# High and low parts written in natural token order, with the un-interleaving moved to the copies of the sums

## The chip, the cores and the metric

The kernel runs on one core of a Trainium2 chip. The metric is the device time of one execution in microseconds, and the median of several executions is compared. One profiled execution gives the trace in which all durations of this text stand. The engines are named as the profile names them: PE (TensorE, with PEld for its weight loads), DVE (VectorE), ACT (ScalarE), POOL (GpSimd) and SP (SyncE, which issues DMAs).

## What is computed

An attention over channels is followed by two feed-forward layers over 6016 tokens of 256 channels, with 2048 hidden channels each:

```python
def _attn_ref(q, k, v, tau):                # B, N, C = 1, 6016, 256
    qn = q / (np.linalg.norm(q, axis=1, keepdims=True) + 1e-06)
    kn = k / (np.linalg.norm(k, axis=1, keepdims=True) + 1e-06)
    s = kn.transpose(0, 2, 1) @ qn / tau
    s = s - s.max(-1, keepdims=True)
    a = np.exp(s)
    a /= a.sum(-1, keepdims=True) + 1e-09
    return (v @ a).astype(np.float32)

x = attn_out.reshape(6016, 256)
h = x @ w_in;   x = (h * np.cos(h)) @ w_out                  # first layer
h = x @ w_in2;  out = (h * (1 / (1 + np.exp(-h)))) @ w_out2  # second layer
```

## The kernel before

**Stages.** A prologue (the first 70 us or so) forms the scores and folds the attention matrix into the first layer's input weights. Then come the two layers. The tokens are cut into 12 blocks, four of 512 tokens and then eight of 496, in this order in both layers, and the hidden channels into 8 pairs of 128-channel slices. A block and a pair make a unit, so each layer has 96 units.

**High and low parts.** Every operand of a matmul is held as two fp32r tensors, the high part (a rounded copy) and the low part (what the rounding left), and a product is three matmuls: weights high by data high, weights low by data high, weights high by data low. For each unit ACT writes the high part and DVE subtracts it to get the low part.

**First layer, per unit.** PE makes `h` (12 matmuls, line 392). ACT takes the turns of the cosine's argument (L404), DVE reduces it (L405), ACT takes the sine (L412), DVE multiplies (L413) and has the product `t`. One unit later ACT writes `hi` from `t` (L420) and DVE writes `lo` (L421). PE uses them two units later, in 12 matmuls that add to the block's sum `o` in PSUM (L433). The order on each engine is the order of the code; ACT's is L404 of this unit, L420 of the last, L412 of this, and DVE's is L405, L421, L413. Between them stand the decoding of weights (L136 on ACT, L140 to L144 on DVE, L137 to L160 on POOL), the splitting of the next block's input on POOL (L213, L216), and the steps by which the last block's sum becomes the second layer's input.

**Between the layers.** `emit_x2` copies a finished sum out of PSUM (L470, ACT, both channel halves in one instruction), forms four combinations of its quarters, splits all seven forms into `yhi` and `ylo` (L454, L457), and stores them to DRAM.

**Second layer, per unit.** Products follow Winograd's form of Strassen's scheme: 2 x 2 blocks, seven products instead of eight, on half-blocks of 256 or 248 tokens. A unit costs 21 matmuls into `xz` and `ys` and 21 into the block's sums `o` (all L500). ACT applies Silu (L760, L771, L772) and copies seeds (L730, L731, L774). DVE adds (L719, L720) and forms combinations (L443, L448, and L449 on POOL). Then ACT writes `hi` and DVE `lo` of the seven forms in two pieces, the raw three (768 or 744 elements) and the formed four (1024 or 992), on L454 and L457. At the end of a block `emit_out` copies the sums out of PSUM (L562 on ACT, L565 and L566 on DVE), and six steps of adds and stores follow in the next units. `emit_last` does the same for the last block. PE's next sum into the same PSUM tile waits for these copies.

**Token order inside a unit.** `columns` lets a matmul read its data operand from two halves in turn: column 2b is token b of the first half of the stored row, column 2b+1 is token b of the second half. In the kernel before, every high and low part is therefore stored with the even tokens in the first half and the odd tokens in the second, so that the matmul's columns come out in natural order. The writer of a part reads its source with a step of two elements (`turns`) and writes densely (`halves`). The two halves lie half a block apart: 1024 or 992 bytes in the first layer, 512 or 496 in the second.

Of the kernel before, what the change touches and what calls it, by code (L numbers as in the profile page):

```python
# [9 lines left out]
F32 = mybir.dt.float32  # L10
# [4 lines left out]
AF = mybir.ActivationFunctionType  # L15
# [6 lines left out]
CH = C // P  # L22
# [44 lines left out]
def attention_then_two_ffns(ctx: ExitStack, tc: tile.TileContext, qk, vT, tau, w_in1, w_out1, w_in2, w_out2, outT):  # L67
# [115 lines left out]

    def columns(t):
        return t.rearrange("p (h b) -> p b h", h=2)

    def halves(t):
        return t.rearrange("p s (h b) -> p s h b", h=2)

    def turns(t):  # L190
        return t.rearrange("p s (b h) -> p s h b", h=2)
# [223 lines left out]
    def emit_split(u, t):  # L415
        b, m = u
        n = BLOCKS[b][1]
        hi = flat(sc.tile([P, NU, HB], F32R, tag="hi", name=f"hi1_{b}_{m}"))
        lo = flat(sc.tile([P, NU, HB], F32R, tag="lo", name=f"lo1_{b}_{m}"))
        nc.scalar.activation(halves(hi[:, :, :n]), turns(t[:, :, :n]), AF.Copy)  # L420
        nc.vector.tensor_tensor(  # L421
            out=halves(lo[:, :, :n]), in0=turns(t[:, :, :n]), in1=halves(hi[:, :, :n]).bitcast(F32), op=ALU.subtract
        )
        return hi, lo

    def emit_o1(u, parts):
# [24 lines left out]
    RAW, FORMED = slice(0, 3), slice(3, NU)  # L451

    def part_hi(t, hi, sl, c):
        nc.scalar.activation(halves(hi[:, sl, :c]), turns(t[:, 1:][:, sl, :c]), AF.Copy)  # L454

    def part_lo(t, hi, lo, sl, c):
        nc.vector.tensor_tensor(  # L457
            out=halves(lo[:, sl, :c]),
            in0=turns(t[:, 1:][:, sl, :c]),
            in1=halves(hi[:, sl, :c]).bitcast(F32),  # L460
            op=ALU.subtract,
        )

    def emit_x2(b):

        n = BLOCKS[b][1]
        c = n // 2
        t = yp.tile([P, NS, HB], F32, tag="y", name=f"y{b}")
        hi, lo = [yp.tile([P, NU, HB], F32R, tag=f"y{s}", name=f"y{s}{b}") for s in ("hi", "lo")]
        nc.scalar.activation(  # L470
            t[:, :4, :c].rearrange("p (a j) c -> p a j c", a=CH),
            state[1, b][:, :, :n].rearrange("p a (j c) -> p a j c", j=2),
            AF.Copy,
        )
        xs[b] = [dp.tile([P, NU, c], F32, name=f"xs{s}{b}") for s in ("hi", "lo")]

        def store(k, x):
            nc.sync.dma_start(out=xs[b][k], in_=x[:, :, :c].bitcast(F32))


        return [
            lambda: forms_first(t, c),
            lambda: forms_second(t, c, nc.vector),
            lambda: part_hi(t, hi, RAW, c),
            lambda: (part_lo(t, hi, lo, RAW, c), part_hi(t, hi, FORMED, c)),
            lambda: (part_lo(t, hi, lo, FORMED, c), store(0, hi), store(1, lo)),
        ]
# [60 lines left out]
    def add(out, x, y):  # L548
        nc.vector.tensor_tensor(out=out, in0=x, in1=y, op=ALU.add)
# [5 lines left out]
    def emit_out(b):  # L555

        c = BLOCKS[b][1] // 2
        o = state[2, b]
        q = qp.tile([P, NU, HB], F32, tag="q", name=f"q{b}", bufs=1)
        p1, p6, p7, p4, p5, p3, p2 = [q[:, i, :c] for i in range(NU)]  # L560
        to = out_at(b)
        nc.scalar.activation(q[:, :4, :c].rearrange("p (k j) c -> p k j c", k=2), o[0][:, :, :, :c], AF.Copy)  # L562

        def second_tile():
            nc.vector.tensor_copy(q[:, 4:6, :c], o[1][:, 0, :, :c])  # L565
            nc.vector.tensor_copy(p2, o[1][:, 1, 0, :c])  # L566

        def store(e, sl):
            nc.sync.dma_start(out=to[:, e], in_=q[:, sl, :c])

        return [
            second_tile,
            lambda: (add(p6, p1, p6), add(p7, p6, p7)),
            lambda: add(p4, p7, p4),
            lambda: (add(p7, p7, p5), store(0, slice(2, 4))),
            lambda: (add(p6, p6, p5), add(p3, p6, p3)),
            lambda: (add(p2, p1, p2), store(1, slice(5, 7))),
        ]

    def emit_last(b, parts, room):  # L580
# [1 line left out]
        c = BLOCKS[b][1] // 2  # L582
        q = qp.tile([P, NU, HB], F32, tag="q", name=f"q{b}", bufs=1)
        s = {name: state[2, b][t][:, k, j, :c] for name, (t, k, j) in BANKS.items()}
        p1, u2, u3, c22, c21, c12, c11 = [q[:, i, :c] for i in range(NU)]
        to = out_at(b)
        nc.scalar.activation(p1, s["P1"], AF.Copy)
        add(u2, p1, s["P6"])
# [2 lines left out]
        add(c22, u3, s["P5"])  # L591
        add(c21, u3, s["P4"])
        emit_plain((b, NPAIR - 1), parts, room)
        add(c21, c21, room[:, 0, :c])
        add(c22, c22, room[:, 1, :c])
        nc.sync.dma_start(out=to[:, 0], in_=q[:, 3:5, :c])
        add(c11, p1, s["P2"])
        nc.scalar.dma_start(out=to[:, 1, 1], in_=c11)
        add(c12, u2, s["P3"])
        nc.sync.dma_start(out=to[:, 1, 0], in_=c12)  # L600


    def as_forms(t):
# [101 lines left out]
    for j in range(len(units) + LAG2):  # L705
# [73 lines left out]
        if final:  # L779
            hi, lo = hl[j - 1] = [sc.tile([P, NU, HB], F32R, tag=s, name=f"{s}2_{j - 1}") for s in ("hi", "lo")]  # L780
            for sl in (slice(0, 2), slice(2, 4)):
                nc.scalar.activation(halves(hi[:, sl, :c]), turns(t[:, sl, :c]), AF.Copy)
                nc.vector.tensor_tensor(
                    out=halves(lo[:, sl, :c]),
                    in0=turns(t[:, sl, :c]),
                    in1=halves(hi[:, sl, :c]).bitcast(F32),
                    op=ALU.subtract,
                )
        elif p is not None:
            hi, lo = [sc.tile([P, NU, HB], F32R, tag=s, name=f"{s}2_{j - 1}") for s in ("hi", "lo")]  # L790
# [31 lines left out]
```

## Time and profile before

| what | value |
|---|---|
| median of 3 executions | 1060.21 us (1059.69 to 1061.05) |
| the profiled execution's own time | 1060.61 us |
| its span, first to last instruction | 1058.8 us |
| mean granted TensorE clock | 0.993 of full speed |
| PE busy | 1020.2 us, 96% of the span |
| DVE busy | 940.4 us, 89% |
| ACT busy | 807.6 us, 76% |
| POOL busy | 331.2 us, 31% |
| time on the ending chain, PE / DVE / ACT | 66% / 19% / 9% of the span |

A busy PE is not a PE at its best rate, since matmuls are pipelined: what PE loses is read from the waits that it is shown in and from the time per matmul of a stretch. The times of a row are microseconds from the start of the span.

### The profile page before, as it was taken

The page shows a single profiled execution, that of the slowest core. Times are in us where ns is not written, and L with a number is a line of the kernel's source. Part 1 is how long each engine was busy: PE and PEld are TensorE (multiplying, and loading weights), DVE is VectorE, ACT ScalarE, POOL GpSimd, SP SyncE. Part 2 cuts the span into 40 slices and gives each one's busy share as a digit, 9 for nine tenths or more (in the row PEclk, how much of TensorE's full clock was granted, in tenths as well). Part 3 has the DMA queues.
Part 4 walks back from the last instruction along what each step waited for, and adds up shares of the span by engine and source line. Part 5 has one row for each costly group of instructions (what it writes and reads, how often), then busy time and mean ns, then how long its engine had stood idle before and what let it go on. Part 6 is the DMA issues. An engine that isn't in the chain of part 4 may idle for free.

```text
span 1058.8 us, 17011 instructions
## 1 busy us (share of the span) xinstructions
PE 1020.2 (96%) x6593; PEld 939.2 (89%) x6593; DVE 940.4 (89%) x1177; ACT 807.6 (76%) x1182; POOL 331.2 (31%) x301
## 2 busy tenths in 40 slices
PE   8888899999999999999999899999999999999998
PEld 7746788787898998999998799999999999999998
DVE  6989999998999899998778689889999889989997
ACT  6555688786776877777767688888888888888885
POOL 2257755646555466450100011111111111111110
PEclk9999999999999999999999999999999999999999
DMA  9712212243250532532056550220220220222001
GB/s 353 285 67 80 80 41 90 75 160 109 108 184 28 169 122 92 159 122 87 1 206 238 211 209 11 81 87 12 79 88 11 78 88 23 67 88 77 21 11 40
DMA packets 56544, 109.49 MB, mean 103 GB/s; under 512 B 2832, under 2 KB 37648, under 8 KB 56464
## 3 DMA queue, kind: packets, MB, share of 16 engines
q1 hardware_dynamic: 56320, 108.28, 30.2%
q8 instruction: 52, 0.85, 0.3%
q14 instruction: 28, 0.23, 0.1%
q10 hardware_dynamic: 144, 0.13, 0.0%
HBM read 68.75 MB, written 39.65 MB: 102 GB/s over the span
## 4 chain that ended last, share of the span: by engine, by line
PE 66%; DVE 19%; ACT 9%; issue 4%; DMA 1%; SPq 0%; DVEq 0%; ACTq 0%
PE o L433 18%; PE h L392 18%; PE o L500 14%; PE xz L500 8%; PE ys L500 6%; ACT hi L454 4%; DVE lo L421 3%; DVE acc L286 2%; ACT t L760 2%; DVE t L443 2%; DVE t L405 2%; DVE t L413 2%; DVE lo L457 1%; DVE t L719 1%; PE pw L353 1%
## 5 line engine op out<-in xcount | busy, mean ns | idle before, releaser
L457 DVE TENSOR_TENSOR lo<-t,hi 128x744 fp32r<-128x744 f32 (+3 forms) x190 | 212.8, 1121 | 39.0 <-ACT hi L454 37.8
L500 PE MATMUL o<-hi,wo 128*128 128x248 f32 (+1 forms) x1330 | 232.6, 275 | 0.0
L454 ACT ACTIVATE hi<-t 128x744 fp32r<-128x744 f32 (+3 forms) x190 | 208.0, 1095 | 16.9 <-PE o L500 16.0
L449 POOL TENSOR_TENSOR t<-t 128x248 f32<-128x248 f32 (+1 forms) x94 | 67.7, 720 | 468.2 <-DVE t L448 372.4
L500 PEld LDWEIGHTS o<-hi,wo 128*128 128x128 f32 x1330 | 202.2, 192 | 0.0
L392 PE MATMUL h<-xhi,wa 128*128 128x496 f32 (+1 forms) x768 | 195.1, 377 | 3.0 <-DVE wa L361 3.0
L433 PE MATMUL o<-hi,wo 128*128 128x496 f32 (+1 forms) x768 | 196.0, 378 | 0.1
L500 PE MATMUL o<-lo,wo 128*128 128x248 f32 (+1 forms) x665 | 183.2, 275 | 0.0
L392 PEld LDWEIGHTS h<-xhi,wa 128*128 128x128 f32 x768 | 146.1, 190 | 21.6 <-issue 4.3
L433 PEld LDWEIGHTS o<-hi,wo 128*128 128x128 f32 x768 | 146.6, 191 | 17.8 <-POOL wv_wo L147 0.5
L412 ACT ACTIVATE t<-t,half_pi 128x992 f32<-128x992 f32 (+1 forms) x96 | 108.7, 1133 | 63.3 <-DVE t L405 63.1
L404 ACT ACTIVATE t<-h 128x992 int32<-128x992 f32 (+1 forms) x96 | 96.5, 1005 | 77.2 <-PE h L392 64.8
L421 DVE TENSOR_TENSOR lo<-t,hi 128x992 fp32r<-128x992 f32 (+1 forms) x96 | 147.6, 1537 | 5.9 <-ACT hi L420 5.8
L405 DVE SCALAR_TENSOR_TENSOR t<-t,h 128x992 f32<-128x992 int32 (+1 forms) x96 | 114.8, 1195 | 36.9 <-ACT t L404 36.6
L500 PE MATMUL xz<-x2hi,wi 128*128 128x248 f32 (+1 forms) x768 | 144.2, 276 | 0.0
L433 PE MATMUL o<-lo,wo 128*128 128x496 f32 (+1 forms) x384 | 116.2, 385 | 13.8 <-DVE lo L421 13.8
L500 PEld LDWEIGHTS o<-lo,wo 128*128 128x128 f32 x665 | 127.8, 192 | 0.0
L420 ACT ACTIVATE hi<-t 128x992 fp32r<-128x992 f32 (+1 forms) x96 | 124.7, 1299 | 3.5 <-DVE t L413 2.2
L500 PE MATMUL ys<-x2hi,wi 128*128 128x248 f32 (+1 forms) x576 | 115.1, 282 | 7.1 <-ACT u L774 4.5
L413 DVE TENSOR_TENSOR t<-h,t 128x992 f32<-128x992 f32 (+1 forms) x96 | 114.8, 1196 | 4.0 <-ACT t L412 1.2
L500 PEld LDWEIGHTS xz<-x2hi,wi 128*128 128x128 f32 x768 | 117.1, 193 | 0.1
L392 PE MATMUL h<-xlo,wa 128*128 128x496 f32 (+1 forms) x384 | 112.5, 375 | 0.0
(129 smaller groups left out, 1697.7 us busy)
## 6 DMA issues: line engine op xcount, KB each, us to landing
qk<-qk_dram SPq DMA_DIRECT2D x22, 512.0 KB, 8.9
raw_wo<-w_out_dram SPq DMA_DIRECT2D x16, 512.0 KB, 5.1
xshi<-yhi SPq DMA_DIRECT2D x8, 868.0 KB, 6.0
xslo<-ylo SPq DMA_DIRECT2D x8, 868.0 KB, 7.0
x2hi<-xshi SPq DMA_DIRECT2D x8, 868.0 KB, 5.7
x2lo<-xslo SPq DMA_DIRECT2D x8, 868.0 KB, 7.6
wo_dram<-stage_wo SPq DMA_DIRECT2D x7, 896.0 KB, 4.5
wo<-wo_dram SPq DMA_DIRECT2D x7, 896.0 KB, 7.5
```

Source lines behind the costliest of these rows:

```text
L392: nc.tensor.matmul(hp[:, s, :n], lhsT, rhs, start=(i == 0), stop=(i == len(todo) - 1))
L404: nc.scalar.activation(k, hp[:, :, :n], AF.Copy, scale=1.0 / TWO_PI, bias=0.25)
L405: nc.vector.scalar_tensor_tensor(out=t[:, :, :n], in0=k, scalar=-TWO_PI, in1=hp[:, :, :n], op0=ALU.mult, op1=ALU.add)
L412: nc.scalar.activation(t[:, :, :n], t[:, :, :n], AF.Sin, bias=half_pi)
L413: nc.vector.tensor_tensor(out=t[:, :, :n], in0=hp[:, :, :n], in1=t[:, :, :n], op=ALU.mult)
L420: nc.scalar.activation(halves(hi[:, :, :n]), turns(t[:, :, :n]), AF.Copy)
L421: nc.vector.tensor_tensor(out=halves(lo[:, :, :n]), in0=turns(t[:, :, :n]), in1=halves(hi[:, :, :n]).bitcast(F32), op=ALU.subtract)
L433: nc.tensor.matmul(o[:, e, :n], wo1_at(i, f)[:, e * P : (e + 1) * P], columns(parts[k][:, s, :n]), start=(f == 0 and (i, k) == PASSES[0]), ...
L449: eng.tensor_tensor(out=t[:, 7, :c], in0=t[:, 3, :c], in1=t[:, 6, :c], op=ALU.subtract)
L454: nc.scalar.activation(halves(hi[:, sl, :c]), turns(t[:, 1:][:, sl, :c]), AF.Copy)
L457: nc.vector.tensor_tensor(out=halves(lo[:, sl, :c]), in0=turns(t[:, 1:][:, sl, :c]), in1=halves(hi[:, sl, :c]).bitcast(F32), op=ALU.subtract,)
L500: nc.tensor.matmul(out, w[:, p, ka - 1], columns(x[r][:, kb - 1, : out.shape[-1]]), start=(start and i == 0), stop=(stop and i == 2), skip ...
```

## The change

Parts made for each unit are stored in natural token order. ACT and DVE then read `t` densely and write `hi` and `lo` densely, in both layers and in the preparation of the second layer's input. The matmuls read exactly as before, through `columns`, so their output columns in PSUM are now shuffled: column 2b is token b and column 2b+1 is token b plus half the block. The copies of the sums at block ends undo this. They read PSUM with a step of two elements (`turns`, `turn`), or of four in `emit_x2`, which has to put tokens back and leave the even and odd halves that the second layer's input parts still need. The attention's input parts (`split_v`) are made as before.

`emit_x2`'s copy becomes two instructions, one for each channel half. `emit_out`'s two copies on DVE become one. In `emit_last` the adds read PSUM with a step of two. No DMA changes its place or size.

```diff
+    def turn(t):
+        return t.rearrange("p (b h) -> p h b", h=2)
...
-        nc.scalar.activation(halves(hi[:, :, :n]), turns(t[:, :, :n]), AF.Copy)
-        nc.vector.tensor_tensor(
-            out=halves(lo[:, :, :n]), in0=turns(t[:, :, :n]), in1=halves(hi[:, :, :n]).bitcast(F32), op=ALU.subtract
-        )
+        nc.scalar.activation(hi[:, :, :n], t[:, :, :n], AF.Copy)
+        nc.vector.tensor_tensor(out=lo[:, :, :n], in0=t[:, :, :n], in1=hi[:, :, :n].bitcast(F32), op=ALU.subtract)
...
     def part_hi(t, hi, sl, c):
-        nc.scalar.activation(halves(hi[:, sl, :c]), turns(t[:, 1:][:, sl, :c]), AF.Copy)
+        nc.scalar.activation(hi[:, sl, :c], t[:, 1:][:, sl, :c], AF.Copy)
 
     def part_lo(t, hi, lo, sl, c):
         nc.vector.tensor_tensor(
-            out=halves(lo[:, sl, :c]),
-            in0=turns(t[:, 1:][:, sl, :c]),
-            in1=halves(hi[:, sl, :c]).bitcast(F32),
-            op=ALU.subtract,
+            out=lo[:, sl, :c], in0=t[:, 1:][:, sl, :c], in1=hi[:, sl, :c].bitcast(F32), op=ALU.subtract
         )
...
-        nc.scalar.activation(
-            t[:, :4, :c].rearrange("p (a j) c -> p a j c", a=CH),
-            state[1, b][:, :, :n].rearrange("p a (j c) -> p a j c", j=2),
-            AF.Copy,
-        )
+        for a in range(CH):
+            nc.scalar.activation(
+                t[:, 2 * a : 2 * a + 2, :c].rearrange("p j (h b) -> p j h b", h=2),
+                state[1, b][:, a, :n].rearrange("p (b h j) -> p j h b", h=2, j=2),
+                AF.Copy,
+            )
...
-        nc.scalar.activation(q[:, :4, :c].rearrange("p (k j) c -> p k j c", k=2), o[0][:, :, :, :c], AF.Copy)
+        first, second = [t.rearrange("p k j c -> p (k j) c") for t in o]
+        nc.scalar.activation(halves(q[:, :4, :c]), turns(first[:, :, :c]), AF.Copy)
 
         def second_tile():
-            nc.vector.tensor_copy(q[:, 4:6, :c], o[1][:, 0, :, :c])
-            nc.vector.tensor_copy(p2, o[1][:, 1, 0, :c])
+            nc.vector.tensor_copy(halves(q[:, 4:, :c]), turns(second[:, :3, :c]))
...
-                nc.scalar.activation(halves(hi[:, sl, :c]), turns(t[:, sl, :c]), AF.Copy)
+                nc.scalar.activation(hi[:, sl, :c], t[:, sl, :c], AF.Copy)
```

On DVE, at the end of the second layer's first block, the two copies of the second PSUM tile `o_0_1` into `q` stand so before, between the adds of one unit and the low parts of the unit ahead of it:

```order
L720 TENSOR_TENSOR t_10_5036<-ys_4373,p_10_4981 128x256
L565 COPY q_5028<-o_0_1_4553 128x512
L566 COPY q_5028<-o_0_1_4553 128x256
L457 TENSOR_TENSOR lo_9_5031<-t_9_4972,hi_9_5030 128x768
L457 TENSOR_TENSOR lo_9_5031<-t_9_4972,hi_9_5030 128x1024
L443 TENSOR_TENSOR t_10_5036<-t_10_5036 128x512
```

and so in the changed kernel:

```order
L720 TENSOR_TENSOR t_10_5048<-ys_4384,p_10_4993 128x256
L565 COPY q_5040<-o_0_1_4565 128x768
L458 TENSOR_TENSOR lo_9_5043<-t_9_4984,hi_9_5042 128x768
L458 TENSOR_TENSOR lo_9_5043<-t_9_4984,hi_9_5042 128x1024
L444 TENSOR_TENSOR t_10_5048<-t_10_5048 128x512
```

The two copies are one, and nothing else moves. On ACT, at the end of the first layer's first block, the copy of the finished sum `o_0` into `y` stands so before, ahead of the next unit's cosine work:

```order
L136 ACTIVATE wv_wi_892<-raw_wi_786 128x512
L470 ACTIVATE y_919<-o_0_609 128x1024
L404 ACTIVATE t_1_2_938<-h_2_925 128x1024
L420 ACTIVATE hi_1_1_941<-t_1_1_883 128x1024
L412 ACTIVATE t_1_2_938<-t_1_2_938,half_pi 128x1024
```

and so in the changed kernel:

```order
L136 ACTIVATE wv_wi_892<-raw_wi_786 128x512
L469 ACTIVATE y_919<-o_0_609 128x512 x2
L407 ACTIVATE t_1_2_939<-h_2_926 128x1024
L423 ACTIVATE hi_1_1_942<-t_1_1_883 128x1024
L415 ACTIVATE t_1_2_939<-t_1_2_939,half_pi 128x1024
```

The copy is two instructions of half the size in the same place. PE, POOL and SP keep their rows in their order.

## Rows read from the trace of the kernel before

**Rows 1.** The page's first part: busy time, share, instructions of each engine.

```profile
PE 1020.2 (96%) x6593; PEld 939.2 (89%) x6593; DVE 940.4 (89%) x1177; ACT 807.6 (76%) x1182; POOL 331.2 (31%) x301
```

**Rows 2.** Windows: length, busy us (instructions) of PE, PEld, DVE, ACT, POOL, clock, DMA.

```profile
100.00:126.50 26.50, 21.79 (x96) 17.85 (x97) 26.23 (x25) 16.19 (x15) 20.27 (x17) 1.00 0.25 80
...
252.60:255.80 3.20, 3.20 (x9) 2.56 (x9) 3.20 (x4) 1.87 (x3) 2.95 (x4) 0.50 0.00 0
...
606.00:745.00 139.00, 136.72 (x1160) 131.38 (x1159) 123.09 (x191) 121.89 (x225) 20.06 (x28) 1.00 0.23 80
757.00:1045.00 288.00, 288.00 (x2582) 288.00 (x2581) 262.62 (x439) 246.21 (x501) 43.53 (x61) 1.00 0.17 52
```

**Rows 3.** Waits (total us, times, longest) in 77:131, 131:255, 577:606 and 606:745.

```profile
PEld o L433 <- DVE lo L421: 12.2, 7, 2.4
...
PEld o L433 <- DVE lo L421: 7.1, 8, 2.3
...
PEld ys L500 <- ACT u L774: 5.0, 4, 2.2
...
PEld ys L500 <- ACT u L774: 7.6, 28, 0.4
```

**Rows 4.** Groups by form: shapes, count, busy us, mean ns, idle before.

```profile
L420 ACT ACTIVATE hi<-t 128x992 fp32r<-128x992 f32 x64 | 74.0, 1156 | 2.6 <-DVE t L413 1.9
L420 ACT ACTIVATE hi<-t 128x1024 fp32r<-128x1024 f32 x32 | 50.7, 1584 | 0.8 <-DVE t L413 0.2
L454 ACT ACTIVATE hi<-t 128x1024 fp32r<-128x1024 f32 x32 | 44.3, 1385 | 0.0
L457 DVE TENSOR_TENSOR lo<-t,hi 128x1024 fp32r<-128x1024 f32 x32 | 41.4, 1295 | 16.3 <-ACT hi L454 15.8
L413 DVE TENSOR_TENSOR t<-h,t 128x1024 f32<-128x1024 f32 x32 | 38.8, 1214 | 1.3 <-ACT t L412 1.2
L412 ACT ACTIVATE t<-t,half_pi 128x1024 f32<-128x1024 f32 x32 | 36.8, 1151 | 31.3 <-DVE t L405 31.3
L281 ACT ACTIVATE sq<-qk 128x1024 f32<-128x1024 f32 x22 | 23.2, 1057 | 10.0 <-DMA qk<-qk_dram 5.9 <-DVE acc L286 4.1
```

**Rows 5.** ACT in order of time, around the step from 512-token to 496-token blocks.

```profile
242.04 0.88 ACT L136 ACTIVATE wv_wi<-raw_wi 128x512 f32<-128x512 f32 x1
...
252.97 1.16 ACT L420 ACTIVATE hi<-t 128x1024 fp32r<-128x1024 f32 x1 [0.23 <-DVE t L413]
...
263.90 1.49 ACT L420 ACTIVATE hi<-t 128x992 fp32r<-128x992 f32 x1
...
266.29 0.68 ACT L136 ACTIVATE wv_wi<-raw_wi 128x512 f32<-128x512 f32 x1
```

**Rows 6.** Chain that ended last, one unit of the second layer's second block.

```profile
661.26 0.63 ACT t L760
661.89 1.30 ACT hi L454
...
663.22 1.29 DVE lo L457
...
666.27 0.63 ACT t L760
```

**Rows 7.** DVE in order of time, a unit of the first layer's first block.

```profile
111.74 1.49 DVE L421 TENSOR_TENSOR lo<-t,hi 128x1024 fp32r<-128x1024 f32 x1
```

**Rows 8.** A block end of the second layer: ACT's copy, PE's next sum.

```profile
638.73 1.07 ACT L562 ACTIVATE q<-o 128x1024 f32<-128x1024 f32 x1
...
640.04 0.39 PE L500 MATMUL o<-hi,wo 128*128 128x256 f32 x2
```

**Rows 9.** Groups by form: copies of sums at block ends.

```profile
L470 ACT ACTIVATE y<-o 128x992 f32<-128x992 f32 x8 | 7.8, 980 | 1.9 <-PE o L433 1.9
...
L565 DVE COPY q<-o 128x512 f32<-128x512 f32 x4 | 2.7, 681 | 0.0
L566 DVE COPY q<-o 128x256 f32<-128x256 f32 x4 | 1.7, 414 | 0.0
```

More of the change, by code (lines that the diff above doesn't have):

```diff
@@ L584, in emit_last @@
         s = {name: state[2, b][t][:, k, j, :c] for name, (t, k, j) in BANKS.items()}
-        p1, u2, u3, c22, c21, c12, c11 = [q[:, i, :c] for i in range(NU)]
+        s = {name: turn(t) for name, t in s.items()}
+        p1, u2, u3, c22, c21, c12, c11 = [q[:, i, :c].rearrange("p (h b) -> p h b", h=2) for i in range(NU)]
         to = out_at(b)
@@ L593, in emit_last @@
         emit_plain((b, NPAIR - 1), parts, room)
-        add(c21, c21, room[:, 0, :c])
-        add(c22, c22, room[:, 1, :c])
+        add(c21, c21, turn(room[:, 0, :c]))
+        add(c22, c22, turn(room[:, 1, :c]))
         nc.sync.dma_start(out=to[:, 0], in_=q[:, 3:5, :c])
         add(c11, p1, s["P2"])
-        nc.scalar.dma_start(out=to[:, 1, 1], in_=c11)
+        nc.scalar.dma_start(out=to[:, 1, 1], in_=q[:, 6, :c])
         add(c12, u2, s["P3"])
-        nc.sync.dma_start(out=to[:, 1, 0], in_=c12)
+        nc.sync.dma_start(out=to[:, 1, 0], in_=q[:, 5, :c])
     def as_forms(t):
@@ L781, in attention_then_two_ffns @@
             for sl in (slice(0, 2), slice(2, 4)):
-                nc.scalar.activation(halves(hi[:, sl, :c]), turns(t[:, sl, :c]), AF.Copy)
+                nc.scalar.activation(hi[:, sl, :c], t[:, sl, :c], AF.Copy)
                 nc.vector.tensor_tensor(
[L784 to L787, printed above, removed]
+                    out=lo[:, sl, :c], in0=t[:, sl, :c], in1=hi[:, sl, :c].bitcast(F32), op=ALU.subtract
                 )
```

## Prediction

> **What bounds the kernel now.** The page's first part comes first [rows 1]: PE is busy 96% of the span, so only what PE loses can be won. Where it loses is read from windows, stretch by stretch [rows 2]. In the second layer's 496-token blocks (757 to 1045) PE is busy 288.00 of 288.00 us with 2582 matmuls, 111.5 ns each, and a unit of 42 matmuls takes 4.68 us. In its 512-token blocks (606 to 745) 1160 matmuls take 139.00 us, 119.8 ns each or 5.03 us a unit. At the rate of the later stretch the 1160 would take 129.4 us, so up to **9.6 us** are lost there; if a matmul's time grew with its columns (256 for 248) they would take 133.5 and 5.5 would be lost.
>
> The list of waits names who makes PE wait [rows 3]. In the first layer it is DVE's low part (L421): 12.2 us in 7 waits up to 131 us, and 7.1 us in 8 waits from 131 to 255. In the second layer it is ACT's seed copy (L774): 5.0 us in 4 waits around the change of layers, and 7.6 us in 28 waits from 606 to 745. All of these lie beside 512-token blocks, and the last sum speaks for the larger loss. Behind them stand ACT and DVE, which shows in the chain of a second-layer unit [rows 6]: Silu (L760), the high part (L454), the low part (L457), then DVE's forms and adds back to the next Silu, 666.27 − 661.26 = 5.01 us, the unit's time. So the loop through L454 and L457 sets the pace there, not PE.
>
> **What strided reading costs.** The groups by form [rows 4] show the parts' instructions slow where the blocks are large. L420 takes 1156 ns for 992 elements and 1584 for 1024; L454 takes 1385 and L457 1295 for 1024. Dense instructions of the same size do not: L412 takes 1151 ns and L413 1214 in the same stretch, and L281, dense on ACT before any of this, 1057. That it is the reading, and what PE reads at that moment, and not the instruction's own size, is shown in order of time [rows 5]. The weight decode L136 also reads with a step of two, always 512 elements. It takes 0.88 us beside 512-token blocks and 0.68 beside 496-token ones. L420 with 992 elements takes 1.49 us at 263.90, while PE still adds up the last 512-token units, and with 1024 elements only 1.16 at 252.97, when the granted clock is 0.50, the 1.2 GHz level [rows 2], and PE works at half the pace. Halves 1024 (or 512) bytes apart thus seem to collide with strided reads; 992 (or 496) do not. In the changed kernel PE reads as before, but the writers of parts read densely, as L412 and L413 do.
>
> I therefore price the dense parts of 1024 elements at **1.06 us on ACT** (L281; 1.15 from L412 is the dear end, whose function differs) and **1.22 on DVE** (L413).
>
> **The change part by part**, against the profiled execution's 1060.61 us, 0.4 above the median.
>
> *Second layer, 512-token blocks.* The loop loses 1.385 − 1.06 = 0.33 us on ACT and 1.295 − 1.22 = 0.08 on DVE: 5.01 − 0.41 = 4.60, under PE's 4.68. PE then sets the pace and nearly all of the 9.6 us goes. In about nine units of this stretch DVE also carries two adds or the block-end copies; I leave 0.08 us for each, as much as DVE itself gains, so 0.7 us stay. **−8.9 us.** If the dense ACT price is 1.15, the loop is 4.70 and the gain about 8.5; if DVE stays as slow as now and ACT gains half, 6.
>
> *First layer, up to 131 us.* DVE is busy 26.23 of 26.50 us [rows 2], since the weight decode stands beside every unit. DVE alone sets the pace, and L421 goes from 1.49 [rows 7] to 1.22: 0.27 in each of 7 waits. **−1.9 us** (−1.1 if two or three of the waits are POOL's doing; −3.5 if the earlier high part counts as well).
>
> *First layer, 131 to 255 us.* The low part comes earlier by 1.584 − 1.06 = 0.52 on ACT and 0.27 on DVE, 0.8 in all. The longest wait, 2.3, keeps 1.5; the other seven share 4.8 and keep about 0.4. **−5.2 us** of 7.1 (−3 if DVE's blocking by POOL decides more of them). After the 2.3 us wait the clock was 0.50 for 3.2 us [rows 2], which cost half of that, 1.6. In 100 to 126.5 the clock stayed at 1.00 [rows 2] through waits of the length now left, so I count **−1.6**, with 0 as the other end.
>
> *Between the layers.* Three of the 4 waits (5.0 us) hang behind a 1024-form of L454: 3 × 0.33 = −1.0. L470 in two pieces costs one more fixed start, about 0.1, on this path once. **−0.9 us** (−1.6 to +0.5). The other eleven L470 lie in the first layer, where ACT waits for PE between units.
>
> *496-token blocks.* PE is never idle there, so 0, in the second layer as in the first.
>
> *Copies out of PSUM with a step.* The trace of before has none. From below: dense, L470 0.98 us [rows 9] and L562 1.07 [rows 8]. From above: the worst strided case against the dense one on SBUF, 1584 / 1057 = 1.5. L562 then takes 1.6 us. It ends at 639.80 and PE's next sum starts at 640.04 [rows 8], 0.24 of room, and L562 itself starts 0.33 earlier once L454 is dense: 0.57 of room against 0.53 more. So 0 from either end, for the four ends beside 512-token parts; the seven later ends lie where PE shows no idle time. The DVE copies merge, 0.68 + 0.41 [rows 9] into one; at 1.5 times they grow by less than the same room. I take the dense value for all, because even the dear end stays inside the room, and 0 for the adds after the last matmul (up to +1: five adds of the size of L566, half as dear again).
>
> The sum: −8.9 −1.9 −5.2 −1.6 −0.9 = −18.5, and 1060.6 − 18.5 = **1042 us**.
>
> **The rivals.**
>
> *Strided PSUM reads cost double* (chance 0.12). L562 takes 2.1 us, 1.04 more against 0.57 of room: about 0.47 at each of 11 block ends, 5 us, and one more at the change of layers. 1048 us. For it: no row shows such a read. Against it: PSUM's dense copies are the cheapest of their size. The Trainium skill ("Advanced Engine Details and Errata", Memory Cachelines) says of PSUM that two consecutive elements should be contiguous and that anything else slows matmuls significantly; it gives no figure for a copy, and no run so far shows one.
>
> *They cost so much that the kernel is slower* (0.05). This is the same place with another price. To eat 18.5 us at 11 ends L562 must take 1.07 + 0.57 + 1.68 = 3.3 us, three times the dense one. At four times, 4.3 us, each end costs 2.6 and the time is 1042 + 29 = 1071. Against it: the worst strided read in these rows costs 1.5 times.
>
> *PE's reads have nothing to do with it* (0.07). Then the 1024-forms stay slow for a reason that the change leaves alone, for instance what they write, and only the strided read's own price goes, 1.16 − 1.06 = 0.10 on ACT [rows 4, 5]: 28 × 0.10 in the second layer and 8 × 0.10 in the first, −3.6. 1057 us. Against it: L136 writes something else and shows the same two prices. The Trainium skill ("SBUF — State Buffer", Who interferes with whom) speaks for this rival: only the port pair shared by VectorE and GpSimd causes contention, and TensorE and ScalarE have ports of their own. By that rule L136 would have one price; it has 0.88 and 0.68 [rows 5], so the trace disagrees.
>
> *DVE becomes the bound in the second layer* (0.08). The gain of 8.9 halves: 1047 us. For it: adds and copies crowd some units. Against it: DVE is busy 123.09 of 139.00 us [rows 2], 4.45 of 5.03 in a unit, already under 4.68.
>
> **How the numbers follow.** The forecast has 0.66; a slower end from something unseen 0.02. Its own best case is −3.5 −7.1 −1.6 −1.6 −9.6 = −23.4 (1037); its worst −1.1 −3 +0.5 −6 = −9.6 (1051). The range 1037.5 to 1052 also holds the doubled copies and the DVE bound, and leaves out 1057 and the slower case. About 0.2% can be told from no change. Faster: 0.66 + 0.12 + 0.08 and half of the 1057 case, 0.89. Same: the other half and a little, 0.05. Slower: 0.06.
>
> **What would show it.** After the change L420 should take about 1.06 us and L421 1.22 in the 512-token blocks, the same as their dense neighbours, and L454 and L457 likewise. The unit in the second layer's 512-token blocks should take 4.7 us, with no wait for L774. The waits for L421 after 131 us should be under 2 us in all, and no stretch near 253 us should show the low clock. A copy L562 above 1.65 us with PE waiting at block ends would show the first rivals right. Parts that stay near 1.4 to 1.6 us would break the forecast altogether.

## The result

The changed kernel takes **1042.43 us** (1042.31 to 1045.18 over four runs) against 1060.14 for the kernel before on the same chip: a ratio of 0.984, 95% interval 0.982 to 0.986. The profiled run took 1042.51 us with a span of 1040.7, against 1058.8. The forecast was 1042.

Lines move by a few places: L423 and L424 are now the first layer's high and low part (L420 and L421 before), L455 and L458 the second layer's (L454 and L457), L469 the copy at a first-layer block end (L470), L434 and L499 the matmuls.

First the page's busy times and, below, the shares of the chain that ended last. PE's busy time falls by 10 us, and its share of the chain rises from 66% to 83%: DVE and ACT set the end in far fewer places. The first line answers [rows 1].

```profile
PE 1010.5 (97%) x6593; PEld 936.3 (90%) x6593; DVE 927.2 (89%) x1166; ACT 751.7 (72%) x1194; POOL 326.1 (31%) x301
...
PE 83%; DVE 12%; ACT 2%; DMA 1%; issue 1%; SPq 0%; DVEq 0%; ACTq 0%
```

The groups by form of the changed kernel, which answer [rows 4] and [rows 9] (count, busy us, mean ns, idle before):

```profile
L423 ACT ACTIVATE hi<-t 128x1024 fp32r<-128x1024 f32 x32 | 33.8, 1055 | 1.1 <-DVE t L416 0.7
L455 ACT ACTIVATE hi<-t 128x1024 fp32r<-128x1024 f32 x32 | 33.9, 1060 | 0.0
L458 DVE TENSOR_TENSOR lo<-t,hi 128x1024 fp32r<-128x1024 f32 x32 | 39.2, 1224 | 10.9 <-ACT hi L455 10.7
L424 DVE TENSOR_TENSOR lo<-t,hi 128x1024 fp32r<-128x1024 f32 x32 | 51.6, 1614 | 0.0
L469 ACT ACTIVATE y<-o 128x512 f32<-128x512 f32 x8 | 4.3, 596 | 0.0
L562 ACT ACTIVATE q<-o 128x1024 f32<-128x1024 f32 x4 | 4.3, 1065 | 0.0
L565 DVE COPY q<-o 128x768 f32<-128x768 f32 x4 | 3.8, 948 | 0.0
```

Both high parts went to the dense price, 1584 and 1385 to 1055 and 1060 ns, and L458 from 1295 to 1224. The copies that now read PSUM with a step cost what dense ones did: L562 1065 ns against 1038 dense. L565 takes 948 ns for 768 elements, where two dense copies took 681 and 414. Only L424 stayed dear, with 1614 ns on the mean.

Windows of the changed kernel, as in [rows 2]:

```profile
100.00:126.50 26.50, 23.21 (x96) 19.08 (x96) 26.22 (x25) 14.74 (x16) 20.38 (x17) 0.94 0.25 80
...
246.90:250.10 3.20, 3.20 (x16) 2.57 (x15) 3.12 (x4) 2.76 (x3) 3.04 (x4) 1.00 0.00 0
575.20:577.80 2.60, 2.60 (x16) 2.38 (x15) 0.98 (x1) 0.66 (x2) 0.00 (x0) 1.00 1.02 422
590.00:727.00 137.00, 136.52 (x1217) 136.13 (x1218) 125.98 (x200) 113.71 (x236) 21.24 (x29) 1.00 0.26 93
740.00:1025.00 285.00, 285.00 (x2554) 285.00 (x2554) 259.64 (x428) 230.59 (x496) 43.62 (x61) 1.00 0.17 52
```

In the second layer's 512-token blocks 1217 matmuls take 137.00 us, 112.6 ns each against 119.8. The 496-token blocks keep their pace (111.6 ns). At 246.90, where the low clock stood before, it is now 1.00. In the first block DVE is still the engine without a pause: it is busy 26.22 of 26.50 us.

The waits of TensorE's weight loads (us, times, longest) in 77:131, 131:255 and 570:600, as in [rows 3]. From 600 to 730 none is left.

```profile
PEld o L434 <- DVE lo L424: 11.1, 6, 3.0
...
PEld o L434 <- DVE lo L424: 2.1, 3, 0.9
...
PEld ys L499 <- ACT u L774: 4.0, 4, 1.9
```

Counting the same matmul in both traces and comparing when it starts gives the gain by stretch:

| stretch (times of before) | forecast, us | measured, us |
| --- | --- | --- |
| first layer, up to 131 us | −1.9 | +0.3 |
| first layer, 131 to 256 (waits and clock) | −6.8 | −6.1 |
| first layer, 496-token blocks | 0 | −0.1 |
| between the layers (570 to 609) | −0.9 | −2.5 |
| second layer, 512-token blocks | −8.9 | −9.6 |
| the rest | 0 | −0.1 |
| sum | −18.5 | −18.1 |

The +0.3 of the first row holds something that the change had no part in. At 77 us TensorE was already 1.5 us behind, and the first changed step starts at 81.47. The changed trace has a stretch at the lower clock (0.50, the 1.2 GHz level) just before, where the trace of before has 1.00. From 77 to 131 us the changed kernel then caught up by 1.3 us. The window of the changed kernel, then the same window before:

```profile
71.40:74.60 3.20, 3.20 (x8) 2.35 (x7) 2.52 (x5) 0.40 (x1) 0.47 (x2) 0.50 0.00 0
```

```profile
71.40:74.60 3.20, 3.20 (x13) 2.06 (x12) 3.13 (x6) 1.02 (x1) 0.47 (x2) 1.00 0.00 0
```

### The profile page after: what moved, and what is told of

Its sections match the earlier page's. It is cut to its first block, busy times and chain, and to the rows that moved or that the text cites. A ratio compares the mean times of both kernels' runs of the same rounds, so it can differ in the third digit from the quotient of the medians.

```text
span 1040.7 us, 17012 instructions
## 1 busy us (share of the span) xinstructions
PE 1010.5 (97%) x6593; PEld 936.3 (90%) x6593; DVE 927.2 (89%) x1166; ACT 751.7 (72%) x1194; POOL 326.1 (31%) x301
## 4 chain that ended last, share of the span: by engine, by line
PE 83%; DVE 12%; ACT 2%; DMA 1%; issue 1%; SPq 0%; DVEq 0%; ACTq 0%
PE o L499 20%; PE h L395 20%; PE o L434 20%; PE xz L499 12%; PE ys L499 9%; DVE acc L289 2%; DVE lo L424 2%; DVE t L408 2%; DVE t L416 1%; PE pw L356 1%; DMA qk<-qk_dram 1%; DVE wv_wo L144 1%; DVE wv_wo L140 1%; DVE wv_wo L141 1%; ACT t L407 0%
## 5 line engine op out<-in xcount | busy, mean ns | idle before, releaser
L458 DVE TENSOR_TENSOR lo<-t,hi 128x744 fp32r<-128x744 f32 (+3 forms) x190 | 207.5, 1095 | 34.4 <-ACT hi L455 33.1
L499 PE MATMUL o<-hi,wo 128*128 128x248 f32 (+1 forms) x1330 | 232.6, 275 | 0.0
L455 ACT ACTIVATE hi<-t 128x744 fp32r<-128x744 f32 (+3 forms) x190 | 178.5, 940 | 32.5 <-PE o L499 31.6
L499 PEld LDWEIGHTS o<-hi,wo 128*128 128x128 f32 x1330 | 201.8, 192 | 0.0
L434 PE MATMUL o<-hi,wo 128*128 128x496 f32 (+1 forms) x768 | 193.9, 375 | 0.0
L499 PE MATMUL o<-lo,wo 128*128 128x248 f32 (+1 forms) x665 | 182.9, 275 | 0.0
L434 PEld LDWEIGHTS o<-hi,wo 128*128 128x128 f32 x768 | 145.0, 189 | 17.1
L499 PE MATMUL xz<-x2hi,wi 128*128 128x248 f32 (+1 forms) x768 | 143.7, 275 | 0.0
L424 DVE TENSOR_TENSOR lo<-t,hi 128x992 fp32r<-128x992 f32 (+1 forms) x96 | 141.6, 1474 | 1.2 <-ACT hi L423 1.2
L499 PEld LDWEIGHTS o<-lo,wo 128*128 128x128 f32 x665 | 127.7, 192 | 0.0
L434 PE MATMUL o<-lo,wo 128*128 128x496 f32 (+1 forms) x384 | 114.2, 379 | 9.9 <-DVE lo L424 9.9
L416 DVE TENSOR_TENSOR t<-h,t 128x992 f32<-128x992 f32 (+1 forms) x96 | 114.9, 1197 | 5.6 <-ACT t L415 1.2
L499 PEld LDWEIGHTS xz<-x2hi,wi 128*128 128x128 f32 x768 | 116.6, 192 | 0.1
L499 PE MATMUL ys<-x2hi,wi 128*128 128x248 f32 (+1 forms) x576 | 112.2, 276 | 3.9 <-ACT u L774 3.1
L499 PE MATMUL xz<-x2lo,wi 128*128 128x248 f32 (+1 forms) x384 | 105.6, 275 | 0.0
```

The source lines that it names most:

```text
L416: nc.vector.tensor_tensor(out=t[:, :, :n], in0=hp[:, :, :n], in1=t[:, :, :n], op=ALU.mult)
L424: nc.vector.tensor_tensor(out=lo[:, :, :n], in0=t[:, :, :n], in1=hi[:, :, :n].bitcast(F32), op=ALU.subtract)
L434: nc.tensor.matmul(o[:, e, :n], wo1_at(i, f)[:, e * P : (e + 1) * P], columns(parts[k][:, s, :n]), start=(f == 0 and (i, k) == PASSES[0]), ...
L455: nc.scalar.activation(hi[:, sl, :c], t[:, 1:][:, sl, :c], AF.Copy)
L458: nc.vector.tensor_tensor(out=lo[:, sl, :c], in0=t[:, 1:][:, sl, :c], in1=hi[:, sl, :c].bitcast(F32), op=ALU.subtract)
L499: nc.tensor.matmul(out, w[:, p, ka - 1], columns(x[r][:, kb - 1, : out.shape[-1]]), start=(start and i == 0), stop=(stop and i == 2), skip ...
```

## The experiments

Each is timed against the kernel before on the same chip, and profiled once.

### The two halves of the change

The first kernel takes over the first layer's parts and the copy between the layers only.

```diff
-        nc.scalar.activation(halves(hi[:, :, :n]), turns(t[:, :, :n]), AF.Copy)
+        nc.scalar.activation(hi[:, :, :n], t[:, :, :n], AF.Copy)
...
-            lambda: part_hi(t, hi, RAW, c),
+            lambda: new_hi(t, hi, RAW, c),
```

> The change in the first layer alone: the parts of the first layer's units and of the second layer's input are written densely and L470's copy undoes the shuffle; the second layer's units write their parts with a strided read as before. Theory (strided reads collide with PE's reading of halves 1024 or 512 bytes apart): the part of L420 takes 1.06 us at 1024 elements, the waits for low parts from 131 us on fall from 7.1 to about 2 us, the second layer's 512-token units stay at 5.0 us with L454 at 1.38. Time 1060.1 minus 6 to 8.5, so 1051.5 to 1054. Rival (all of the gain is in the second layer's loop, and the first layer's only moves its waits): 1058 or more.

Measured: 1052.99 us, ratio 0.992 (0.990 to 0.994), as the theory expected. The second kernel takes over the second layer's units and their copies at block ends only.

```diff
-        nc.scalar.activation(halves(hi[:, sl, :c]), turns(t[:, 1:][:, sl, :c]), AF.Copy)
+        nc.scalar.activation(hi[:, sl, :c], t[:, 1:][:, sl, :c], AF.Copy)
...
-            lambda: part_hi(t, hi, RAW, c),
+            lambda: old_hi(t, hi, RAW, c),
```

> The change in the second layer's units alone: the first layer and the copy between the layers are as before. Theory: L454 takes 1.06 us at 1024 elements, a 512-token unit of the second layer 4.69 us and no wait for L774 from unit to unit; L420 stays at 1.58 and the waits for low parts up to 255 us at 19 us. Time 1060.1 minus 9.5 to 11, so 1049 to 1050.6. If the two halves of the change are independent, its gain and that of the first layer alone add up to about 18. Rival (the loop is taken over by DVE): unit 4.85 us or more, 1054 or more.

Measured: 1050.05 us, ratio 0.989 (0.987 to 0.990), again as expected. Together the halves give 8.1 + 11.1 = 19.2 us of medians, the whole 17.7: they add, within the spread of such differences.

The second kernel also shows something about the clock. Its first layer is that of before, and near 250 us TensorE waits as it did before (2.4 us; before 2.3). Yet the clock stays at 1.00 behind the wait, where before it fell to 0.50 [rows 2], and from 131 to 256 us this kernel gains 1.6 us on the one before. The wait between 247 and 256 us, and a window behind it:

```profile
PEld o L436 <- DVE lo L424: 2.4, 1, 2.4
...
254.60:257.80 3.20, 3.20 (x17) 2.86 (x16) 3.20 (x4) 1.93 (x3) 2.95 (x4) 1.00 0.00 0
```

### Is it the dense read, or the distance that TensorE reads over?

If two places 1024 or 512 bytes apart, read in turn by TensorE, are what hurts a copy with a step of two, then other distances must cure it with the copies left as they were. The kernel before, with other block sizes alone:

```diff
-SIZES = 4 * [512] + 8 * [496]
+SIZES = 4 * [504] + 8 * [500]
```

> The kernel before with one number changed: twelve blocks of 504 and 500 tokens (four and eight) in place of 512 and 496, so that the halves that PE reads in turn lie 1008 or 1000 bytes apart in the first layer and 504 or 500 in the second. All writers of parts still read with a step of two. Theory (the collision needs halves a power of two apart): L420 takes 1.15 to 1.20 us for 1008 elements, L136 0.68 everywhere, second-layer units 4.7 us, time 1043 to 1047. Rival (a strided read is slow because the piece is large, or because of what stands beside the first four blocks): L420 stays near 1.5, time 1058 to 1061.

Measured: **1042.28 us**, ratio 0.981 (0.980 to 0.983), a little below the theory's range. The forms of this kernel, with the strided copies of before:

```profile
L420 ACT ACTIVATE hi<-t 128x1008 fp32r<-128x1008 f32 x32 | 37.2, 1162 | 1.0 <-DVE t L413 0.7
L454 ACT ACTIVATE hi<-t 128x1008 fp32r<-128x1008 f32 x32 | 37.1, 1159 | 0.0
```

1008 elements take 1162 ns where 1024 took 1584. One line of sizes gives the whole gain without any dense copy, so reading with a step of two costs about 0.1 us by itself (1162 against 1055), and the rest is the meeting with TensorE.

Size and distance change together there. The next two kernels part them, in the first layer only: its tiles have room, so the halves can be laid at any distance. First 1056 bytes in every block, those of 512 tokens too:

```diff
+    PAD = 8
+
+    def spaced(t):
+        w = HB + PAD
+        return t.rearrange("p s c -> p (s c)")[:, : 4 * w].rearrange("p (s h w) -> p s h w", s=2, h=2)
...
-        nc.scalar.activation(halves(hi[:, :, :n]), turns(t[:, :, :n]), AF.Copy)
+        nc.scalar.activation(hi[:, :, :, : n // 2], turns(t[:, :, :n]), AF.Copy)
...
-                columns(parts[k][:, s, :n]),
+                spaced_columns(parts[k], s, n),
```

> The kernel before with blocks of 512 and 496 and strided writers as they were, but in the first layer the two halves of every row of parts lie 1056 bytes apart instead of 1024 (and 992 in blocks of 496). Theory (it is the distance of the two places that TensorE reads in turn): the high part of 1024 elements in the first layer falls from 1.58 us to 1.15 to 1.20, and the first layer's gain of the half change comes back without dense writers: 1050 to 1055 us; the second layer keeps its 139 ns per matmul in 512-token blocks. Rival (it is the number of elements, or the tile's size): 1.58 us stays and the time is 1059 to 1062 us.

Measured: 1051.02 us, ratio 0.992 (0.990 to 0.994), the same as the first half of the change (0.992), with strided copies and blocks of 512. (The 139 in that expectation is the length of the second layer's stretch in us. A matmul took 119.8 ns there before.) Then the converse, 1024 bytes in every block, those of 496 tokens too:

```diff
-    PAD = 8
+    PAD = 0
```

> The kernel before with strided writers and its own block sizes, but in the first layer the two halves of a row of parts start 1024 bytes apart in every block, those of 496 tokens too (992 before). Theory (the distance decides, not the number of tokens): the high part of 992 elements in the first layer rises from 1.16 us to 1.4 to 1.6, next to that of 1024 elements, which stays at 1.58; the time stays at 1060 to 1066 us, since those blocks have no wait of TensorE that ends at the parts as long as they come within a unit. Rival (the size decides): 992 elements stay at 1.15 to 1.17 us and the time at 1059 to 1062 us.

Measured: 1069.62 us, ratio 1.008 (1.006 to 1.010). The forms of the first (L429 at 1056 bytes, L463 the second layer's at its old 512 bytes) and of the second:

```profile
L429 ACT ACTIVATE hi<-t 128x1024 fp32r<-128x1024 f32 x32 | 37.9, 1186 | 1.1 <-DVE t L422 0.7
L463 ACT ACTIVATE hi<-t 128x1024 fp32r<-128x1024 f32 x32 | 44.5, 1391 | 0.0
```

```profile
L429 ACT ACTIVATE hi<-t 128x992 fp32r<-128x992 f32 x64 | 96.0, 1501 | 2.2 <-DVE t L422 1.8
L429 ACT ACTIVATE hi<-t 128x1024 fp32r<-128x1024 f32 x32 | 50.3, 1572 | 0.8 <-DVE t L422 0.4
...
PEld o L442 <- DVE lo L430: 18.5, 19, 2.6
```

At 1056 bytes 1024 elements cost 1186 ns; at 1024 bytes 992 elements cost 1501, against 1156 at 992 bytes [rows 4]. So the distance decides, not the size. The time of the converse was missed by 4 us: I had counted the 496-token units as wide enough, but some of them, behind a weight decode, now make TensorE wait (the last row, 131 to 570 us; before it was 8.2 us in 11 waits there).

The changed kernel with the new sizes asks whether the two cures add.

```diff
-SIZES = 4 * [512] + 8 * [496]
+SIZES = 4 * [504] + 8 * [500]
```

> The changed kernel with four blocks of 504 and eight of 500 tokens in place of 512 and 496. Theory: dense copies and a distance that is no power of two are two ways out of one collision, so they don't add: 1039 to 1043 us. Rival: each takes away a cost of its own of some 18 us and they add: 1022 to 1030 us.

Measured: **1040.0 us**, ratio 0.981 (0.979 to 0.983). They don't add, so they cure one thing. This is the lowest time of all, but its interval touches that of the change (0.982 to 0.986), and the two were not timed side by side.

### Which side of the copy, and which reader

ScalarE can also go through the tokens in order and write to the two halves in turn. What lies in memory afterwards is the same.

```diff
-        nc.scalar.activation(halves(hi[:, :, :n]), turns(t[:, :, :n]), AF.Copy)
+        nc.scalar.activation(dealt(hi[:, :, :n]), pairs(t[:, :, :n]), AF.Copy)
```

(`dealt` and `pairs` put the half innermost; the second layer's line is edited alike.)

> The kernel before, but ScalarE goes through the tokens of a high part in natural order: it reads the data densely and writes in turn to the two halves; the result in memory is the same, VectorE's low parts are as before. Theory A (the step of two on ScalarE's reading side meets TensorE's reads): the high parts of 1024 elements fall to 1.05 to 1.20 us and the time to 1042 to 1048 us. Rival B (any access of ScalarE in steps meets them, writing too): 1.4 us and more stays, and the time is 1057 us or above, above 1062 if writing to two places 1024 bytes apart is worse than reading in steps.

Measured: 1151.19 us, ratio 1.086 (1.084 to 1.089). Its forms:

```profile
L426 ACT ACTIVATE hi<-t 128x992 fp32r<-128x992 f32 x64 | 127.2, 1987 | 2.7 <-DVE t L419 2.2
L426 ACT ACTIVATE hi<-t 128x1024 fp32r<-128x1024 f32 x32 | 66.7, 2086 | 1.1
L460 ACT ACTIVATE hi<-t 128x1024 fp32r<-128x1024 f32 x32 | 65.8, 2056 | 0.0
```

Writing in turn to two places costs 2.0 ns an element at any distance seen (1987 / 992, 2086 / 1024), nearly double the dense price, and 92 us of time. Theory A missed. The numbers are those of rival B, but not for its reason: 992 elements pay as much as 1024, so this is a price of its own and not the collision. It left no way to see whether a dense read cures the collision here. The changed kernel itself is that test, with 1055 ns.

If TensorE reads the tiles front to back, the collision should vanish from the other side. The writers stay as they were, so tokens come to the sums in another order and nothing puts them back: only the time of this kernel is of use.

```diff
     def columns(t):
-        return t.rearrange("p (h b) -> p b h", h=2)
+        return t
```

> The kernel before with one line changed: matmuls read their data operand in the order in which it is stored and not from two halves in turn, so the tokens of a block come out in another order; the writers of parts still read with a step of two. Theory (it takes both: strided readers and PE reading in turn from halves a power of two apart): L420 takes 1.15 to 1.16 us at 1024 elements, L136 0.67 everywhere, second-layer 512-token units 4.7 us, time 1043 to 1047. Rival (strided reads are slowed by any reading of PE): L420 above 1.4 us, time near 1060.

Measured: 1086.79 us, ratio 1.023 (1.022 to 1.025): both theories missed. The collision did go, as the first row below shows. What cost 26 us was open, so the next kernel makes the writers dense as well.

```diff
     def columns(t):
-        return t.rearrange("p (h b) -> p b h", h=2)
+        return t

     def halves(t):
-        return t.rearrange("p s (h b) -> p s h b", h=2)
+        return t

     def turns(t):
-        return t.rearrange("p s (b h) -> p s h b", h=2)
+        return t
```

> All parts in natural order and TensorE reading them front to back as well: every reader and writer is dense. Theory: what cost 26 us in the run with TensorE reading densely is TensorE's own pace (in its trace 1105 matmuls in the 250 us from 300 on against 1193 before, so 226 ns each against 210; in the second layer 114.0 ns against 111.8), and who writes the parts and how doesn't matter to it. Then this kernel lies at 1080 to 1087 us, with the high part of 1024 elements at 1.05 us. Rival: the slow pace came from dense TensorE reads meeting the writers' steps of two; then with dense writers the pace is back at 210 and 111.8 ns and the time at 1038 to 1046 us.

Measured: 1085.05 us, ratio 1.024 (1.022 to 1.026): the theory held. The form of the first of these two kernels, then windows of TensorE (length, busy, matmuls, clock) of the second, then the same windows of the kernel before:

```profile
L420 ACT ACTIVATE hi<-t 128x1024 fp32r<-128x1024 f32 x32 | 36.4, 1138 | 0.2
```

```profile
300.00:550.00 250.00, 250.00 (x1105) 1.00 0.30 98
...
740.00:1020.00 280.00, 280.00 (x2457) 1.00 0.19 59
```

```profile
300.00:550.00 250.00, 249.72 (x1193) 1.00 0.34 113
...
740.00:1020.00 280.00, 279.94 (x2504) 1.00 0.20 60
```

TensorE is busy all through these windows (at most 0.3 us short), and the clock is full, yet a matmul of 496 columns takes 226.2 ns (250.00 / 1105) when read front to back and 209.3 when read from two halves in turn; one of 248 columns takes 114.0 against 111.8. Over 1536 matmuls of the first kind, and the second layer's 4032 all priced as the second kind, that is 26 + 9 = 35 of the 42.6 us that lie between this kernel and the change. The rest lies in the 512-token blocks and was not taken apart. So how the parts are written has no say in it: matmuls that read front to back are slower here. Whether they would be so without the other engines at work, no run shows. The order of halves in the kernel before buys the faster pace, and the change keeps it.

### The first block

The one term that failed was the first block. There DVE and POOL decode weights beside every unit. In the changed kernel the low part still takes 1.49 us there, and 1.22 where POOL is idle. DVE and POOL in order of time (start, us): a unit of the first block, a later unit with POOL idle, and a later one beside a longer POOL step:

```profile
111.20 1.30 POOL L147 TENSOR_TENSOR wv_wo<-wv_wo,raw_wo 128x512 int32<-128x512 int32 x1 [1.32 <-DVE wv_wo L144]
112.10 1.49 DVE L424 TENSOR_TENSOR lo<-t,hi 128x1024 fp32r<-128x1024 f32 x1
112.59 1.47 POOL L150 TENSOR_SCALAR wo<-wv_wo 128x512 fp32r<-128x512 f32 x1
...
156.18 1.22 DVE L424 TENSOR_TENSOR lo<-t,hi 128x1024 fp32r<-128x1024 f32 x1
...
185.73 2.10 POOL L160 TENSOR_TENSOR stage_wi<-wv_wi,stage_wi 128x896 fp32r<-128x896 f32 x1
186.08 2.83 DVE L424 TENSOR_TENSOR lo<-t,hi 128x1024 fp32r<-128x1024 f32 x1
```

I took L150 for the step that costs the low part its time. So this copy was moved to ScalarE, one unit later:

```diff
+        def finish(self):
+            if self.pending is not None:
+                v, hi, lo = self.pending
+                self.pending = None
+                nc.scalar.activation(hi, v, AF.Copy)
+                nc.gpsimd.tensor_tensor(out=lo, in0=v, in1=hi.bitcast(F32), op=ALU.subtract)
...
-                nc.gpsimd.tensor_scalar(out=hi, in0=v, scalar1=1.0, scalar2=1.0, op0=ALU.mult, op1=ALU.mult)
-                nc.gpsimd.tensor_tensor(out=lo, in0=v, in1=hi.bitcast(F32), op=ALU.subtract)
+                self.pending = (v, hi, lo)
```

> The changed kernel, with the rounded high part of the first layer's second weights made by ScalarE one unit later instead of by GpSimd. Theory: in block 0 VectorE has no idle time and its low part takes 1.49 us, against 1.22 in later blocks, because GpSimd's copy runs beside it (112.59 to 114.06 us beside 112.10 to 113.59 in the trace of the changed kernel); without the copy the low part takes 1.2 to 1.3 us in block 0, eight units gain about 0.2 us each, and the time is 1040 to 1041.5 us. Rival: the low part is slowed by GpSimd's other operations (the subtraction that stays is 1.3 us long) or the copy on ScalarE delays its other steps; then 1042 to 1044 us.

Measured: 1045.17 us, ratio 0.986 (0.985 to 0.988): a miss. Its rows:

```profile
101.36 1.48 DVE L431 TENSOR_TENSOR lo<-t,hi 128x1024 fp32r<-128x1024 f32 x1
...
100.46 1.30 POOL L155 TENSOR_TENSOR wv_wo<-wv_wo,raw_wo 128x512 int32<-128x512 int32 x1 [1.16 <-DVE wv_wo L152]
...
PEld o L441 <- POOL wo L124: 4.6, 1, 4.6
```

Without L150 the low part still takes 1.48: the wrong step was taken away. L155 here is L147 of the changed kernel. It runs until 101.76 and has 0.40 us left when the low part starts, as in the rows above (until 112.50, the low part from 112.10). The price follows that remainder. In the changed kernel's first layer 25 low parts of 512-token units start while a POOL step runs, and each takes what is left of that step and 1.08 us more, within 0.04: 0.40 + 1.08 for 1.49 us, 1.75 + 1.08 for 2.83. A POOL step that starts during the low part, as L150 does, adds nothing to it. Moving L147 itself was not tried.

TensorE also meets a new wait of 4.6 us for the weights' low part, which stands in POOL's queue behind the input of the second block and its transfer. Two kernels go on from there. One takes that wait away and splits the input four units later:

```diff
-            load_v(1)
+            WO1.finish()
+            vraw1 = load_v(1, split=False)
...
+            if m == 4:
+                split_v(1, vraw1, nc.scalar)
```

> The changed kernel with the rounded copy of the first layer's second weights on ScalarE, as in the run before this one that lost 1.8 us to it, but with the copy's low part put ahead of the input of block 1 in GpSimd's queue, and that input split four units later with its high part on ScalarE. Theory (that run lost because GpSimd stood 5.15 us at the input's transfer with the weights' low part queued behind it, and TensorE waited 4.24 us for that part; otherwise the copy saves VectorE time in block 0): the 4.24 us wait is gone and the time is 1037 to 1041 us. Rival (VectorE's steps in block 0 are slowed by whatever GpSimd runs, and moving it about gives nothing): 1041.5 to 1044 us.

The other is the change with the later split alone.

```diff
-            load_v(1)
+            vraw1 = load_v(1, split=False)
...
+            if m == 4:
+                split_v(1, vraw1, nc.scalar)
```

> The changed kernel with only the split of block 1's input put four units later and its high part on ScalarE. Theory: the waits of 2.2 and 2.7 us and the stretch at 1.2 GHz near 100 us come from GpSimd's long operations on that input (1.61 and 2.83 us) beside VectorE's low parts (2.29 and 2.11 us there); put later, TensorE's waits in block 0 fall by 1 to 3 us: 1039.5 to 1041.5 us. Rival: VectorE meets the same operations four units on, and pays there: 1042 to 1044 us.

Measured: 1042.88 us, ratio 0.984 (0.982 to 0.986), and 1041.24 us, 0.982 (0.980 to 0.984). The first is its rival's case: the 4.6 us wait is gone, and a wait for the high part stands in its place. The second came into its theory's range, but it can't be told from the change (0.982 to 0.986). Its theory's reason is not borne out either: TensorE still waits 11.0 us for low parts from 77 to 131 (11.1 in the change), and DVE meets POOL's long step four units on, as its rival said. A wait of the first, then DVE and POOL of the second:

```profile
PEld o L441 <- ACT hi L430: 3.4, 2, 3.2
```

```profile
111.61 2.53 DVE L141 TENSOR_SCALAR wv_wo<-wv_wo 128x512 int32<-128x512 int32 x1
...
111.23 2.62 POOL L219 TENSOR_TENSOR xlo<-vraw,xhi 128x1024 fp32r<-128x1024 f32 x1
```

So moving these POOL steps about gives the time nothing that can be measured. That DVE's low part stands behind the POOL step under way is shown by the rows; that less work for the two together would speed the block was not tried.

## Why the prediction was right, and where its steps were off

**The loop of the second layer** was right. Its dense prices came out as taken, 1060 ns for 1.06 us and 1224 for 1.22, the waits for L774 are gone, and a unit of 42 matmuls takes 42 × 112.6 = 4.73 us. The 0.7 us that I kept back for units with adds and copies was not lost: the stretch gave 9.6 for 8.9.

**The first layer from 131 us** was right in its waits: the high part at 1055 ns, the low part at 1.22 us where POOL is idle, and waits from 7.1 to 2.1 us. It gave 6.1 of 6.8. Of this 1.7 us is the stretch at 1.2 GHz that did not come, and that part is luck as far as the runs show: the kernel with only the second layer changed kept the wait of 2.4 us, and its clock stayed up all the same (one profiled execution of each). So the step from a shorter wait to a kept clock is not shown. Over the whole trace the clock came out as forecast by balance: after 60 us before has three low stretches (92, 253 and 580 us), the changed kernel two (71 and 102), and those at 71, 253 and 580, counted matmul for matmul, cost 1.7 us each.

**The first block** failed: forecast −1.9, measured +0.3. The failed step is "L421 goes from 1.49 to 1.22". The row was taken as the price of a strided read, but dense reading leaves 1.49 there: it is the price of POOL at work beside DVE, which the change doesn't touch. Before, too, the low part at 111.74 [rows 7] started 0.41 us before the end of L147 (110.84 to 112.15), and 0.41 + 1.08 is its 1.49. The step of two cost nothing there, which fits: TensorE was waiting for this very part [rows 3]. The row gave no reason to choose one cause over the other; what did give one was the POOL column of the same window, 20.27 us busy of 26.50 [rows 2], which I passed over. The low parts of the block set its pace and came 6.6 us apart before and after; the 1.3 us between 77 and 131 are a late start made up. The mean of L424 stays at 1614 ns for the same reason. The Trainium skill ("SBUF — State Buffer", Who interferes with whom) has a rule for such a price: a VectorE instruction with two inputs in SBUF contends with GpSimd's reads. The rows agree, 1.49 against 1.22 us.

**Between the layers** was too small: 2.5 for 0.9. The waits themselves gave about what was forecast. L470 in two pieces cost 0.16 more (2 × 596 against 1030 ns), taken as about 0.1. The rest is the clock. After the same wait of 2.6 us for the first layer's last product (L413, now L416) the kernel before ran at 1.2 GHz until 583.70, and the changed one didn't (575.20 above). The row of before, which I hadn't read:

```profile
581.20:583.70 2.50, 2.50 (x8) 2.11 (x8) 0.98 (x1) 0.66 (x2) 0.00 (x0) 0.50 1.01 422
```

Matmul for matmul, from 580 to 584 us, the changed kernel gained 1.7 us here. Both half-kernels kept a low stretch near this place, and no run shows what decides it, so this gain too is luck. In the first block the changed kernel has one at another place than before (92 us there), so there it gave nothing back:

```profile
102.20:105.00 2.80, 2.80 (x8) 2.21 (x7) 2.73 (x4) 0.82 (x1) 1.56 (x3) 0.50 0.20 71
```

**Copies out of PSUM with a step** were priced at nothing beyond the dense copy, and cost nothing: 1065 against 1038 ns. Both rivals on that copy fall with it. DVE didn't become the bound either.

**The rival that TensorE's reads have nothing to do with it** falls on the two kernels with spaced halves: the same instruction on the same number of elements costs 1572 or 1186 ns, as the halves lie 1024 or 1056 bytes apart. The Trainium skill ("SBUF — State Buffer", Who interferes with whom) also says that TensorE and ScalarE never wait on anyone; these rows disagree, and the measurement decides.

## What to carry over

When one instruction has two prices, look at what another engine reads at that moment before counting its elements: here a step-of-two copy on ScalarE lost 0.4 us to TensorE reading over 1024 bytes, and 8 tokens fewer in a block cured it as well as a rewritten layout. A price read beside a second suspect (POOL here) is no price until a row without it is found; here the step to suspect was the one already under way when the slow one started. And before straightening an odd access order, ask which engine it serves: making all of it dense made this kernel 2.4% slower.

## What the runs showed of the hardware

- A copy on ScalarE that reads every second float from SBUF costs 1.16 us for 1008 elements, dense 1.06 for 1024. While TensorE reads in turn from two places 1024 bytes apart, it costs 1.50 (992) to 1.58 us (1024), at 512 bytes 1.39. At 992, 1000, 1008 and 1056 bytes there is no such loss. What sets 512 and 1024 apart is open.
- A copy on ScalarE that writes in turn to two places in SBUF costs 2.0 ns an element, at every distance seen.
- A copy that reads PSUM with a step of two costs the dense price on ScalarE (1065 against 1038 ns for 1024 elements).
- A DVE subtraction of two operands in SBUF (128x1024) that starts while a POOL step runs takes what is left of that step and 1.08 us more, in 25 of 25 cases within 0.04 us; with POOL idle it takes 1.22.
- After the same wait of TensorE near 250 us (2.3 and 2.4 us) the granted clock fell to 0.50 in one kernel and stayed at 1.00 in another with the same first layer. Each such stretch cost 1.7 us, counted matmul for matmul.
- TensorE takes 226.2 ns for 496 fp32r columns read front to back and 209.3 read from two halves in turn, at the full clock. Why is open.
